# A fused attention and two-MLP kernel: state products 64 columns at a time, scores over the update in PSUM, and tile 0 in another order

## The chip, the core and the metric

The kernel runs on one core of a Trainium2 chip. The metric is the device time of one execution in microseconds (us); times are medians over runs. The engines are PE (TensorE, matrix products), PEld (its weight loads), DVE (VectorE), ACT (ScalarE), POOL (GpSimd) and SP (SyncE, which here only issues DMAs). Each works through its own queue in program order and waits for the others through semaphores.

## The reference

A gated linear attention over 4 batches, 8 heads, 768 tokens, head size 32 and state size 16, then two MLPs of width 256 to 2048 to 256 on the 3072 tokens.

```python
for c in range(nc):                       # chunks of the sequence
    cum = np.cumsum(la, axis=-1)
    L = np.exp(cum[:, :, :, None] - cum[:, :, None, :]) * causal
    M = np.einsum('bhin,bhjn->bhij', Cc, Bc) * L
    y_intra = np.einsum('bhij,bhjd->bhid', M, xc)
    y_inter = np.einsum('bhin,bhnd->bhid', Cc, state) * np.exp(cum)[:, :, :, None]
    y[:, :, sl] = y_intra + y_inter
    state = decay_full * state + sum_j(B_j x_j * decay_from_j)
...
h = np.maximum(x @ w_in, 0.0);  x = h * h @ w_out              # first MLP
h = x @ w_in2;  out = (h * np.clip(h + 3, 0, 6) / 6) @ w_out2  # second MLP
```

## The kernel before

The tokens stand as 6 tiles of 512 (128 tokens of each batch). Every large product is made from a high and a low part of both operands, in three terms: high by high, low by high, high by low. The attention runs in 12 *levels* of 64 tokens for all batches and heads; two levels make one tile.

The first MLP is a loop over tiles t = 0..5 and 16 blocks f = 0..15 of the hidden width. One pass is a *step* (t, f), written out by `step` (line 553). It puts into the queues, in this order: `mm1` (line 513, six matmuls of 512 columns) into one of two PSUM buffers; ACT's relu (522); in tile 0 for the blocks in `SQUARE` also ACT's square (524); `ready`, the splitting of a weight half into its high part on ACT (470) and its low part on POOL (472); DVE's square where ACT did not make it (528); the *burst*, attention work on PE; `mm2` of the step two before (546, six matmuls); ACT's high part `gha` (530); the *mid*, attention work of the other engines and, in tile 0, the decoding of a weight half; DVE's low part `gla` (532), which `mm2` of this step needs two steps later.

One level l of the attention is:

- `scale` (282, POOL): the rows B and C times their decays; `head` (291, ACT): C by head into `cb`; `tok` (297, POOL): B by token times its decay.
- `state` (PE, burst): a new tile `att` of four PSUM banks; `inter` (328), C by the state, into columns 256 to 383 (`y`), and `update` (356), B by x, into `u`, columns 384 to 511.
- `chunk` (PE, burst): `intra` (342), the masked scores of this level by x, added to `y`; then `scores` (308) of the level l+1 into columns 0 to 255 of the same tile.
- `high` (382, ACT) and `low` (387, DVE): `y` copied out as the high and low part of the MLP's input.
- `adv` (367 and 369, DVE): the next state from `u` and the old one.
- `mask` (316, DVE): the scores of the next level copied under the causal mask into `mt`, two banks in each of two instructions.

The tile `att` has one buffer only: `state` of level l+1 writes where `mask` l+1 reads the scores and `high`, `low` and `adv` of level l read `y` and `u`. The scheduler puts semaphore waits between accesses of two engines to one bank of one tile.

The order is written out by hand. `PLAN` says which of these stand at which step of tiles 0 to 2. From level 4 on a level has four steps: at 4l `mask` l, `tok` l and `scale` l+1; at 4l+1 `head` l+1; at 4l+2 `state` l; at 4l+3 `chunk`, `high`, `adv` and the loads of level l+2; at 4l+4 `low`. In tile 0 `JOIN1` says at which step a weight half j is decoded on DVE (`join`: `sign` 433, `bits` 438, `merge` 443), after ACT's `early` (429) a step before and ahead of its split a step later. Halves 2f' and 2f'+1 are the first and second MLP matrix of blocks 2f' and 2f'+1. A raw half of 512 KB comes by DMA (418) into places that the activations use later (halves 2 to 9) or into a ring of two buffers `raw` (the others).

Of the kernel before, what the change touches and what calls it, by code (L numbers as in the profile page):

```python
# [18 lines left out]
P = 128  # L19
NB = 4  # L20
H = 8
HD = 32
# [6 lines left out]
CH = 64  # L29
G = 256  # L30
# [12 lines left out]
NQUAD = NPAIR * NQ  # L43
LASTATT = 2

PLAN = {0: {0: ("upd1", "scale2"), 1: ("load3", "adv1", "head2"), 3: ("first2", "scale3"),
            4: ("mask2", "tok2", "head3"), 5: ("state2",), 6: ("chunk2", "adv2"), 7: ("high2", "load4"), 8: ("low2",),
            9: ("mask3", "tok3", "scale4"), 10: ("head4",), 11: ("state3",), 12: ("chunk3",), 13: ("high3", "load5"),
            14: ("low3", "gammas0"), 15: ("adv3",)}}
for _l in range(4, 12):  # L50
    for _k, _v in ((0, (f"mask{_l}", f"tok{_l}", f"scale{_l + 1}")), (1, (f"head{_l + 1}",)), (2, (f"state{_l}",)),
                   (3, (f"chunk{_l}", f"high{_l}", f"adv{_l}", f"load{_l + 2}")), (4, (f"low{_l}",))):
        _d = PLAN.setdefault((4 * _l + _k) // 16, {})
        _f = (4 * _l + _k) % 16
        _d[_f] = _v + _d.get(_f, ()) if _k == 4 else _d.get(_f, ()) + _v

JOIN1 = {0: 4, 1: 5, 2: 6, 3: 7, 5: 8, 6: 9, 7: 10, 8: 11, 10: 12, 11: 13, 12: 14, 13: 15}

SQUARE = (0, 2, 3, 5, 6, 7, 8, 9, 11)
QKEEP = 3
QNEW = 4

# [8 lines left out]
def attn_mlp_mlp(ctx: ExitStack, tc, a, bT, cT, bK, x, w1i, w1o, w2i, w2o, yT):  # L73


    nc = tc.nc
# [18 lines left out]
    act_h, act_l = {}, {}  # L95
# [147 lines left out]
    lev = [dict() for _ in range(NLEV)]  # L243
    state = {}

    def load(l, ec=nc.sync, eb=nc.sync):
        if l >= NLEV:
            return
        lev[l]["bc"] = t = at2.tile([P, NB, 2, CH], F32, tag="bc", name=f"bc{l}")
        for i, (eng, src) in enumerate(((ec, cT), (eb, bT))):  # L250
            eng.dma_start(out=t[:, :, i], in_=src.rearrange("p (b s) -> p b s", b=NB)[:, :, l * CH:l * CH + CH])

    def load_x(l, ex=nc.sync, eb=nc.sync):
        if l >= NLEV:
            return
        lev[l]["xb"] = t = at2.tile([P, 2, DM + P], F32, tag="xb", name=f"xb{l}")
        for eng, src, cols in ((eb, bK, slice(DM, DM + P)), (ex, x, slice(0, DM))):
            for r in range(2):
                eng.dma_start(out=t[CH * r:CH * r + CH, :, cols],
                              in_=src.rearrange("t (b l) w -> t b l w", b=NB)[:, 2 * r:2 * r + 2, l, :])  # L260

    def load_ef(l):
        if l >= NLEV:
            return
        s, k = divmod(l, CPG)
        lev[l]["ef"] = e = at2.tile([P, NB, 2 * CH], F32, tag="ef", name=f"ef{l}")
        nc.sync.dma_start(out=e.rearrange("p b t -> p (b t)"), in_=scr[k, s].rearrange("h b w t -> h (b w t)")
                          .unsqueeze(1).broadcast_to([H, NS, 2 * G]))

    def load_all(l):  # L270
        load(l)
        load_x(l)
        load_ef(l)

    def scale(l, eng=None):

# [40 lines left out]
                                      tri.bitcast(U32).unsqueeze(1).unsqueeze(1).broadcast_to([P, 2, NB, CH]),  # L317
                                      sc[:, q].rearrange("p k (z i) -> p k z i", i=CH))

    def inter(l, m=HD):  # L320

        y, d = lev[l]["y"], lev[l]
        for b in range(NB):
            for p in range(NPR):
                q, (r, c) = slice(32 * p, 32 * p + 32), divmod(b, 2)
                for e in range(0, 2 * HD, m):
                    o = CH * (p % 2) + e
                    nc.tensor.matmul(out=y[o:o + m, 2 * r + p // 2, c * CH:c * CH + CH],  # L328
                                     lhsT=state["S"][q, b, e:e + m], rhs=d["bc"][q, b, 0], start=c == 0,
                                     stop=False, skip_group_check=True)  # L330

    def intra(l):

# [39 lines left out]
    def operand(l, k):  # L373

        return act(l // 2, k).rearrange("p k (b l i) -> p k b l i", b=NB, l=2)[:, :, :, l % 2]

    def outputs(l, r):
        return lev[l]["y"][:, 2 * r:2 * r + 2].rearrange("p k (c i) -> p k c i", c=2)

    def evac_h(l):  # L380
        for r in range(2):
            nc.scalar.copy(out=operand(l, "h")[:, :, 2 * r:2 * r + 2], in_=outputs(l, r))

    def evac_l(l):
        for r in range(2):
            hi, lo = (operand(l, k)[:, :, 2 * r:2 * r + 2] for k in "hl")
            nc.vector.tensor_tensor(out=lo, in0=outputs(l, r), in1=hi.bitcast(F32), op=ALU.subtract)  # L387

    def place(l, t):
        lev[l].update(t=t, y=t[:, :, G:G + P], u=t[:, :, G + P:])  # L390

    def from_state(l):

# [11 lines left out]
    class Weights:  # L405
# [4 lines left out]
            self.raw, self.low, self.wt, self.v, self.hi, self.lo = {}, {}, {}, {}, {}, {}  # L410

        def dma(self, j):
            if self.pre == "a" and 2 <= j < 10:
                t, k = ((1, "h"), (2, "h"), (3, "h"), (3, "l"), (4, "h"), (4, "l"), (5, "h"), (5, "l"))[j - 2]
                raw = actp.tile([P, 2, 256, 2], U32, tag=f"{k}{t}", name=f"rawa{j}")
            else:
                raw = stagep.tile([P, 2, 256, 2], U32, tag="raw", name=f"raw{self.pre}{j}", bufs=2)
            nc.sync.dma_start(out=raw, in_=self.src[j % 2][:, j // 2].bitcast(U32).rearrange("p k (n w) -> p k n w", w=2))
            self.raw[j] = raw.rearrange("p k n w -> p (k n) w")
# [82 lines left out]
    w = {}  # L502
    pend = []

    def mm1(pre, t, f):
        ih, il, _, _ = w[pre].parts
        fb, fo = divmod(f, 2)
        pool, tag = (ps_y, "y") if 16 * t + f >= 52 and f % 4 > 1 else (ps_h, "h")
        h = pool.tile([P, TOK], F32, tag=tag, name=f"h{pre}{t}_{f}")
        i = 0  # L510
        for k in range(2):
            for wt, xt in ((ih, act_h), (il, act_h), (ih, act_l)):
                nc.tensor.matmul(out=h, lhsT=wt[fb][:, k, fo * P:fo * P + P], rhs=xt[t][:, k, :],  # L513
                                 start=i == 0, stop=i == 5)
                i += 1
        return h

    def gate(pre, t, f, h):
        gh = mlpp.tile([P, TOK], F32R, tag="gh", name=f"gh{pre}{t}_{f}", bufs=3)
        gl = mlpp.tile([P, TOK], F32R, tag="gl", name=f"gl{pre}{t}_{f}", bufs=3)  # L520
        g = mlpp.tile([P, TOK], F32, tag="g", name=f"g{pre}{t}_{f}")
        nc.scalar.activation(out=g, in_=h, func=AF.Relu)  # L522
        if t == 0 and f in SQUARE:
            nc.scalar.activation(out=g, in_=g, func=AF.Square)
            yield
        else:
            yield
            nc.vector.tensor_tensor(out=g, in0=g, in1=h, op=ALU.mult)  # L528
        yield
        nc.scalar.activation(out=gh, in_=g, func=AF.Copy)  # L530
        yield
        nc.vector.tensor_tensor(out=gl, in0=g, in1=gh.bitcast(F32), op=ALU.subtract)  # L532
        yield gh, gl
# [19 lines left out]

    def step(pre, t, f, ready=None, mid=None):

        gt = gate(pre, t, f, mm1(pre, t, f))
        next(gt)
        if ready:
            ready()
        next(gt)  # L560
        if t <= LASTATT + 1:
            burst_of(t, f)
        if len(pend) == LAG:
            mm2(*pend.pop(0))
        next(gt)
        if mid:
            mid(t, f)
        pend.append((pre, t, f, *next(gt)))
# [217 lines left out]
    w1 = w["a"] = Weights(w1i, w1o, "a")  # L786
# [52 lines left out]
    evac_h(0)  # L839
    evac_l(0)  # L840
    place(1, ps_a.tile([P, NPR, TOK], F32, tag="att", name="att1"))
    inter(1, 2 * HD)
    intra(1)
    w1.join(1)
    w1.early(2)
    w1.join(2)
    evac_h(1)
    evac_l(1)
    w1.split(1)
    w1.early(3)  # L850
    w1.split(2)
    w1.join(3)
# [13 lines left out]
    def attention(t, f, on_pe):  # L866
        for nm in PLAN.get(t, {}).get(f, ()):
            k = nm.rstrip("0123456789")
            l = int(nm[len(k):])
            if (k in ("state", "chunk", "first", "upd")) == on_pe and (l < NLEV or k in ("load", "scale", "head")):  # L870
                does[k](l)

    def burst_of(t, f):
        attention(t, f, True)
# [3 lines left out]
    def ready():  # L878

        if todo:  # L880
            x, j = todo.popitem()
            x.split(j)

    def decode(plan, f):
        if f in plan:
            w1.join(plan[f])
            todo[w1] = plan[f]
        if f + 1 in plan and plan[f + 1] not in w1.v:
            w1.early(plan[f + 1])
# [3 lines left out]
    def mid_first(t, f):  # L893
        attention(t, f, False)
        decode(JOIN1, f)
        for j in {0: (6, 7), 1: (8,), 2: (9,), 3: (10, 11), 7: (12,), 8: (13,), 10: (14,), 11: (15,)}.get(f, ()):
            w1.dma(j)

    def mid(t, f):
        attention(t, f, False)  # L900
        run(16 * t + f, 0)
# [92 lines left out]
```

## Time and profile before

| | |
|---|---|
| median of 3 runs | 584.66 us (584.62 to 585.59) |
| the profiled execution: its time | 586.12 us |
| the profiled execution: span of the trace | 584.4 us |
| PE busy | 562.1 us, 96% |
| DVE busy | 420.2 us, 72% |
| ACT busy | 359.3 us, 61% |
| POOL busy | 143.1 us, 24% |

How to read it: a busy share is an average over the span. The question for each stretch is whether PE waits there, and for whom. PEclk is the granted clock of PE: 1.00 is 2.4 GHz and 0.50 is 1.2 GHz. In the timeline the start and the duration are followed by the instruction; in square brackets stands the idle time of the engine before it, and what ended that. A matmul's duration contains the drain of the array, so the pace of a row of matmuls is read from start to start.

### The profile page before, as it was taken

The numbers are of one execution on the slowest core, as the hardware profiler recorded it, in microseconds if no ns is written. First come the engines' busy times: TensorE is split into PE (matmuls) and PEld (weight loads), VectorE is DVE, ScalarE is ACT, GpSimd is POOL, SyncE is SP. The second block draws the span as 40 slices with busy tenths as digits, with TensorE's granted clock in tenths as the row PEclk, the third lists the DMA queues.
The fourth block names the chain that finished last, engine by engine and source line by source line (L and its number), as shares of the span: only waits on it lengthen the run. The fifth ranks groups of instructions, "written<-read, shape, count | busy, mean of one in ns | idle before, by whom it ended". The sixth has DMA issues, their size and how long they took to land.

```text
span 584.4 us, 11106 instructions
## 1 busy us (share of the span) xinstructions
PE 562.1 (96%) x4451; PEld 449.4 (77%) x4451; DVE 420.2 (72%) x663; ACT 359.3 (61%) x624; POOL 143.1 (24%) x195
## 2 busy tenths in 40 slices
PE   7789899999999999999999899999999999999996
PEld 4457677777777888888887688888788888788885
DVE  6896786665565677667776876887867878676774
ACT  4576645444444565665665776777766777666663
POOL 6372550111210144344247400330000600000000
PEclk9799999999999999999999999999999999999999
DMA  8863412222240122122211000000200000200002
GB/s 239 224 211 101 127 47 60 70 65 66 65 136 3 37 73 60 49 72 73 72 37 36 1 1 1 1 0 1 72 1 1 1 1 0 72 1 0 1 1 73
DMA packets 32803, 31.47 MB, mean 54 GB/s; under 512 B 14608, under 2 KB 27376, under 8 KB 32752
## 3 DMA queue, kind: packets, MB, share of 16 engines
q1 hardware_dynamic: 30352, 29.85, 17.9%
q10 hardware_dynamic: 2400, 0.92, 0.6%
q8 instruction: 35, 0.57, 0.4%
q14 instruction: 16, 0.13, 0.1%
HBM read 27.41 MB, written 3.35 MB: 53 GB/s over the span
## 4 chain that ended last, share of the span: by engine, by line
PE 84%; POOL 4%; DVE 4%; ACT 3%; issue 3%; DMA 2%; POOLq 0%; DVEq 0%; ACTq 0%
PE y L691 22%; PE ha L513 19%; PE ya L546 18%; PE X L646 11%; PE Z L646 6%; PE V L646 3%; PE att L342 1%; DMA rawa<-in_w1o 1%; POOL al L472 1%; PE att L328 1%; PE att L308 1%; ACT ga L522 1%; POOL wtb L452 1%; PE att L356 1%; POOL bl L498 1%
## 5 line engine op out<-in xcount | busy, mean ns | idle before, releaser
L532 DVE TENSOR_TENSOR gla<-ga,gha 128x512 fp32r<-128x512 f32 x96 | 75.6, 787 | 32.3 <-ACT gha L530 32.0
L530 ACT ACTIVATE gha<-ga 128x512 fp32r<-128x512 f32 x96 | 60.6, 632 | 60.3 <-DVE ga L528 60.3
L522 ACT ACTIVATE ga<-ha 128x512 f32<-128x512 f32 x96 | 56.9, 593 | 61.1 <-PE ha L513 60.8
L528 DVE TENSOR_TENSOR ga<-ga,ha 128x512 f32<-128x512 f32 x87 | 59.6, 685 | 41.9 <-ACT ga L522 41.6
L513 PE MATMUL ha<-act_h,ah 128*128 128x512 f32 x192 | 76.2, 397 | 2.6 <-ACT ah L470 1.7
L513 PE MATMUL ha<-act_l,ah 128*128 128x512 f32 x192 | 76.1, 396 | 2.7 <-DVE act_l L387 2.7
L546 PE MATMUL ya<-gha,ah 128*128 128x512 f32 x192 | 77.9, 406 | 0.0
L513 PE MATMUL ha<-act_h,al 128*128 128x512 f32 x192 | 76.2, 397 | 0.8 <-POOL al L472 0.8
L546 PE MATMUL ya<-gla,ah 128*128 128x512 f32 x192 | 75.7, 394 | 1.4 <-DVE gla L532 1.4
L546 PE MATMUL ya<-gha,al 128*128 128x512 f32 x192 | 75.2, 392 | 0.0
L677 DVE TENSOR_TENSOR glc<-c,ghc 128x512 fp32r<-128x512 f32 x96 | 67.6, 706 | 5.7 <-ACT ghc L674 4.3
L668 DVE SCALAR_TENSOR_TENSOR c<-rc,c 128x512 f32<-128x512 f32 x72 | 50.9, 708 | 23.7 <-ACT rc L660 23.4
L660 ACT ACTIVATE rc<-c,three 128x512 f32<-128x512 f32 x72 | 52.0, 722 | 24.7 <-DVE c L655 24.5
L691 PE MATMUL y<-ghc,bh 128*128 128x512 f32 x168 | 65.5, 390 | 0.0
L691 PE MATMUL y<-glc,bh 128*128 128x512 f32 x168 | 65.4, 389 | 0.0
L691 PE MATMUL y<-ghc,bl 128*128 128x512 f32 x168 | 65.4, 389 | 0.0
L674 ACT ACTIVATE ghc<-c 128x512 fp32r<-128x512 f32 x96 | 58.7, 630 | 3.4 <-DVE c L668 3.2
L655 DVE TENSOR_TENSOR c<-Z,u 128x512 f32<-128x512 f32 x48 | 33.1, 690 | 22.8 <-PE Z L646 22.0
L513 PEld LDWEIGHTS ha<-act_h,ah 128*128 128x128 f32 x192 | 36.6, 191 | 11.3 <-ACT ah L470 2.5
L513 PEld LDWEIGHTS ha<-act_l,ah 128*128 128x128 f32 x192 | 36.8, 191 | 10.6 <-DVE act_l L387 3.1
L546 PEld LDWEIGHTS ya<-gla,ah 128*128 128x128 f32 x192 | 36.3, 189 | 10.6 <-DVE gla L532 3.0
L513 PEld LDWEIGHTS ha<-act_h,al 128*128 128x128 f32 x192 | 36.6, 191 | 9.8 <-POOL al L472 2.2
(297 smaller groups left out, 1022.6 us busy)
## 6 DMA issues: line engine op xcount, KB each, us to landing
rawa<-in_w1i SPq DMA_DIRECT2D x8, 512.0 KB
rawa<-in_w1o SPq DMA_DIRECT2D x8, 512.0 KB
rawb<-in_w2i SPq DMA_DIRECT2D x8, 512.0 KB
rawb<-in_w2o SPq DMA_DIRECT2D x8, 512.0 KB
xb<-in_x SPq DMA_DIRECT2D x24, 128.0 KB
ef<-scr SPq DMA_DIRECT2D x10, 256.0 KB
out_yT<-xf SPq DMA_DIRECT2D x10, 256.0 KB
bc<-in_cT SPq DMA_DIRECT2D x12, 128.0 KB
```

The lines of the kernel that those rows point to most:

```text
L513: nc.tensor.matmul(out=h, lhsT=wt[fb][:, k, fo * P:fo * P + P], rhs=xt[t][:, k, :], start=i == 0, stop=i == 5)
L522: nc.scalar.activation(out=g, in_=h, func=AF.Relu)
L528: nc.vector.tensor_tensor(out=g, in0=g, in1=h, op=ALU.mult)
L530: nc.scalar.activation(out=gh, in_=g, func=AF.Copy)
L532: nc.vector.tensor_tensor(out=gl, in0=g, in1=gh.bitcast(F32), op=ALU.subtract)
L546: nc.tensor.matmul(out=ys[m], lhsT=terms[i][0][fb][:, fo, m * P:m * P + P], rhs=terms[i][1], start=f == 0 and i == 0, stop=f == NF - 1 and ...
L646: nc.tensor.matmul(out=self.ps[bank], lhsT=lhsT, rhs=rhs, start=start and i == 0, stop=stop and i == 2, skip_group_check=True)
L660: nc.scalar.activation(out=self.sb["r" + c], in_=src, func=AF.Relu, bias=three)
L668: nc.vector.scalar_tensor_tensor(out=self.sb[c], in0=self.sb["r" + c], scalar=6.0, in1=src, op0=ALU.min, op1=ALU.mult)
L674: nc.scalar.activation(out=self.gh[c], in_=self.sb[c], func=AF.Copy)
L677: nc.vector.tensor_tensor(out=self.gl[c], in0=self.sb[c], in1=self.gh[c].bitcast(F32), op=ALU.subtract)
L691: nc.tensor.matmul(out=ys[t][m], lhsT=terms[i][0][:, 7 + 2 * (1 - f) + m], rhs=terms[i][1], start=first and i == 0, stop=last and i == 2, ...
```

## The change

`inter` always takes 64 columns of the state in one product (before: 32 at a time, except at level 1, which the call `inter(1, 2 * HD)` ran at 64). `u` moves to columns 0 to 127 of `att`, where `scores` of the next level are put later, so `adv` of a level has to be ahead of its `chunk` in the plan. From level 4 on a level now runs: 4l `state` and `scale` l+1; 4l+1 `adv` and `head` l+1; 4l+2 `chunk` and `tok` l+1; 4l+3 `mask` l+1, `high`, `low` and the loads. In tile 0 `PLAN`, `JOIN1`, `SQUARE` and the steps of the weight DMAs change, halves 12 to 15 land in the places of halves 6 to 9, `mm1` of step (0, 0) takes its two terms with the low input last, and ahead of the loop `low` of level 1 comes before the merge of half 1 and the decoding of half 2. `load_all` issues `ef` ahead of `x`.

```diff
-PLAN = {0: {0: ("upd1", "scale2"), 1: ("load3", "adv1", "head2"), 3: ("first2", "scale3"),
-            4: ("mask2", "tok2", "head3"), 5: ("state2",), 6: ("chunk2", "adv2"), 7: ("high2", "load4"), 8: ("low2",),
-            9: ("mask3", "tok3", "scale4"), 10: ("head4",), 11: ("state3",), 12: ("chunk3",), 13: ("high3", "load5"),
-            14: ("low3", "gammas0"), 15: ("adv3",)}}
+PLAN = {0: {0: ("upd1", "scale2"), 1: ("adv1", "load3", "head2"), 3: ("first2", "scale3", "gammas0"), 4: ("mask2", "tok2"),
+            5: ("head3",), 6: ("state2",), 7: ("adv2", "tok3"), 8: ("chunk2",), 9: ("mask3", "high2", "low2", "load4"),
+            11: ("state3", "scale4"), 12: ("adv3", "head4"), 13: ("chunk3",),
+            14: ("tok4", "mask4", "high3", "low3", "load5")}}
 for _l in range(4, 12):
-    for _k, _v in ((0, (f"mask{_l}", f"tok{_l}", f"scale{_l + 1}")), (1, (f"head{_l + 1}",)), (2, (f"state{_l}",)),
-                   (3, (f"chunk{_l}", f"high{_l}", f"adv{_l}", f"load{_l + 2}")), (4, (f"low{_l}",))):
...
+    for _k, _v in ((0, (f"state{_l}", f"scale{_l + 1}")), (1, (f"adv{_l}", f"head{_l + 1}")), (2, (f"chunk{_l}", f"tok{_l + 1}")),
+                   (3, (f"mask{_l + 1}", f"high{_l}", f"low{_l}", f"load{_l + 2}"))):
...
-JOIN1 = {0: 4, 1: 5, 2: 6, 3: 7, 5: 8, 6: 9, 7: 10, 8: 11, 10: 12, 11: 13, 12: 14, 13: 15}
-SQUARE = (0, 2, 3, 5, 6, 7, 8, 9, 11)
+JOIN1 = {0: 4, 1: 5, 2: 6, 3: 7, 4: 8, 5: 9, 6: 10, 7: 11, 8: 12, 10: 13, 11: 14, 13: 15}
+DMA1 = {0: (6, 7), 1: (8,), 2: (9,), 3: (10, 11), 4: (12,), 5: (13,), 6: (14,), 8: (15,)}
+SQUARE = (0, 2, 3, 4, 6, 8, 10, 11, 13)
...
     def load_all(l):
         load(l)
+        load_ef(l)
         load_x(l)
-        load_ef(l)
...
-    def inter(l, m=HD):
+    def inter(l):
...
-                for e in range(0, 2 * HD, m):
-                    o = CH * (p % 2) + e
-                    nc.tensor.matmul(out=y[o:o + m, 2 * r + p // 2, c * CH:c * CH + CH],
-                                     lhsT=state["S"][q, b, e:e + m], rhs=d["bc"][q, b, 0], start=c == 0,
-                                     stop=False, skip_group_check=True)
+                o = CH * (p % 2)
+                nc.tensor.matmul(out=y[o:o + CH, 2 * r + p // 2, c * CH:c * CH + CH], lhsT=state["S"][q, b],
+                                 rhs=d["bc"][q, b, 0], start=c == 0, stop=False, skip_group_check=True)
...
-        lev[l].update(t=t, y=t[:, :, G:G + P], u=t[:, :, G + P:])
+        lev[l].update(t=t, y=t[:, :, G:G + P], u=t[:, :, 0:P])
...
-            if self.pre == "a" and 2 <= j < 10:
-                t, k = ((1, "h"), (2, "h"), (3, "h"), (3, "l"), (4, "h"), (4, "l"), (5, "h"), (5, "l"))[j - 2]
+            if self.pre == "a" and j >= 2 and j not in (10, 11):
+                t, k = ((1, "h"), (2, "h"), *((t, k) for t in (3, 4, 5) for k in "hl"))[j - 2 if j < 10 else j - 8]
...
-        gt = gate(pre, t, f, mm1(pre, t, f))
+        gt = gate(pre, t, f, mm1(pre, t, f, *(() if t or f else ((0, 1, 3, 4, 2, 5),))))
...
-    inter(1, 2 * HD)
+    inter(1)
     intra(1)
-    w1.join(1)
-    w1.early(2)
-    w1.join(2)
+    w1.sign(1)
+    w1.bits(1)
     evac_h(1)
     evac_l(1)
+    w1.merge(1)
+    w1.early(2)
     w1.split(1)
+    w1.join(2)
     w1.early(3)
...
-        for j in {0: (6, 7), 1: (8,), 2: (9,), 3: (10, 11), 7: (12,), 8: (13,), 10: (14,), 11: (15,)}.get(f, ()):
+        for j in DMA1.get(f, ()):
             w1.dma(j)
```

## Rows read from the trace of the kernel before

**Rows 1.** Busy time by stage: stretch, length, then busy us of each engine, PEclk, DMA share.

```profile
20.04:84.63 64.59, 56.45 (x629) 41.96 (x630) 52.86 (x81) 42.56 (x78) 33.79 (x41) 0.89 0.52 145
84.63:195.00 110.37, 110.37 (x1858) 87.22 (x1857) 66.58 (x113) 51.41 (x99) 15.93 (x20) 1.00 0.22 62
```

**Rows 2.** Waits of PE from 20 to 200 us: total, times, longest.

```profile
PE att L328 <- issue: 2.9, 1, 2.9
PE ha L513 <- DVE act_l L387: 2.7, 1, 2.7
PE ha L513 <- ACT ah L470: 1.7, 1, 1.7
...
PE ha L513 <- POOL al L472: 0.8, 3, 0.3
```

**Rows 3.** Busy time by stage, columns as in rows 1, behind two waits of PE.

```profile
42.00:48.00 6.00, 5.09 (x106) 4.08 (x107) 3.91 (x7) 3.85 (x8) 1.87 (x3) 0.72 0.21 48
70.00:74.00 4.00, 3.83 (x101) 2.41 (x100) 1.80 (x3) 2.23 (x4) 1.66 (x3) 0.58 0.53 155
```

**Rows 4.** Timeline of PE: the state products at 64 columns, then at 32.

```profile
17.71 0.69 PE L328 MATMUL att<-bc,S 32*64 32x64 f32 x32 [0.80 <-DVE S L369]
18.34 0.86 PE L342 MATMUL att<-mt,xb 64*32 64x64 f32 x64
...
104.96 0.39 PE L513 MATMUL ha<-act_l,ah 128*128 128x512 f32 x1
105.28 0.85 PE L328 MATMUL att<-bc,S 32*32 32x64 f32 x64
106.07 0.45 PE L356 MATMUL att<-xb 64*32 64x64 f32 x32
```

**Rows 5.** Timeline of two steps of tile 1, all engines.

```profile
113.44 0.39 PE L513 MATMUL ha<-act_l,ah 128*128 128x512 f32 x1
...
114.56 0.69 DVE L528 TENSOR_TENSOR ga<-ga,ha 128x512 f32<-128x512 f32 x1 [0.95 <-ACT ga L522]
115.03 0.39 PE L513 MATMUL ha<-act_h,ah 128*128 128x512 f32 x1
115.16 0.75 DVE L387 TENSOR_TENSOR act_l<-att,act_h 128x256 fp32r<-128x256 f32 x2
115.83 1.36 DVE L316 COPY_PREDICATED mt<-tri,att 128x512 f32<-128x512 uint32 x2
116.16 0.39 PE L513 MATMUL ha<-act_l,ah 128*128 128x512 f32 x1
```

**Rows 6.** Timeline: `high` and `low` of level 0.

```profile
17.69 0.65 ACT L382 CAST act_h<-yu 128x256 fp32r<-128x256 f32 x2 [3.93 <-DVE S L369]
18.37 0.76 DVE L387 TENSOR_TENSOR act_l<-yu,act_h 128x256 fp32r<-128x256 f32 x2 [0.71 <-ACT act_h L382]
```

**Rows 7.** Waits of DVE, 85 to 200 us: total, times, longest.

```profile
DVE S L367 <- ACT act_h L382: 8.6, 7, 1.2
```

**Rows 8.** DVE by line, 19 to 88 us: count, busy us, mean ns, idle before.

```profile
L532 DVE TENSOR_TENSOR gla<-ga,gha 128x512 fp32r<-128x512 f32 x16 | 13.2, 825 | 0.8 <-ACT gha L530 0.8
L443 DVE SCALAR_TENSOR_TENSOR wta<-wta,lowa 128x512 uint32<-128x512 uint32 x15 | 12.2, 813 | 1.4
L438 DVE TENSOR_SCALAR lowa<-rawa 128x512 uint16<-128x512 uint16 x15 | 9.9, 662 | 0.5
L433 DVE TENSOR_SCALAR lowa<-rawa 128x512 uint32<-128x512 uint32 x15 | 9.4, 627 | 0.1
...
L369 DVE TENSOR_TENSOR S<-S,gam 128x256 f32<-128x256 f32 x3 | 2.3, 772 | 0.1
...
L367 DVE TENSOR_TENSOR S<-att,S 128x256 f32<-128x256 f32 x3 | 1.3, 418 | 4.1 <-PE att L308 4.1
L233 DVE TENSOR_SCALAR gam<-gl,hm 128x32 f32<-128x32 f32 x2 | 1.2, 672 | 0.0
L230 DVE TENSOR_TENSOR gl<-gl 128x44 f32<-128x44 f32 x1 | 0.7, 735 | 0.0
```

More of the change, by code (lines that the diff above doesn't have):

```diff
@@ L44 @@
 LASTATT = 2
-PLAN = {0: {0: ("upd1", "scale2"), 1: ("load3", "adv1", "head2"), 3: ("first2", "scale3"),
-            4: ("mask2", "tok2", "head3"), 5: ("state2",), 6: ("chunk2", "adv2"), 7: ("high2", "load4"), 8: ("low2",),
-            9: ("mask3", "tok3", "scale4"), 10: ("head4",), 11: ("state3",), 12: ("chunk3",), 13: ("high3", "load5"),
-            14: ("low3", "gammas0"), 15: ("adv3",)}}
+PLAN = {0: {0: ("upd1", "scale2"), 1: ("adv1", "load3", "head2"), 3: ("first2", "scale3", "gammas0"), 4: ("mask2", "tok2"),
+            5: ("head3",), 6: ("state2",), 7: ("adv2", "tok3"), 8: ("chunk2",), 9: ("mask3", "high2", "low2", "load4"),
+            11: ("state3", "scale4"), 12: ("adv3", "head4"), 13: ("chunk3",),
+            14: ("tok4", "mask4", "high3", "low3", "load5")}}
 for _l in range(4, 12):
-    for _k, _v in ((0, (f"mask{_l}", f"tok{_l}", f"scale{_l + 1}")), (1, (f"head{_l + 1}",)), (2, (f"state{_l}",)),
-                   (3, (f"chunk{_l}", f"high{_l}", f"adv{_l}", f"load{_l + 2}")), (4, (f"low{_l}",))):
-        _d = PLAN.setdefault((4 * _l + _k) // 16, {})
-        _f = (4 * _l + _k) % 16
-        _d[_f] = _v + _d.get(_f, ()) if _k == 4 else _d.get(_f, ()) + _v
-JOIN1 = {0: 4, 1: 5, 2: 6, 3: 7, 5: 8, 6: 9, 7: 10, 8: 11, 10: 12, 11: 13, 12: 14, 13: 15}
-SQUARE = (0, 2, 3, 5, 6, 7, 8, 9, 11)
+    for _k, _v in ((0, (f"state{_l}", f"scale{_l + 1}")), (1, (f"adv{_l}", f"head{_l + 1}")), (2, (f"chunk{_l}", f"tok{_l + 1}")),
+                   (3, (f"mask{_l + 1}", f"high{_l}", f"low{_l}", f"load{_l + 2}"))):
+        PLAN.setdefault((4 * _l + _k) // 16, {})[(4 * _l + _k) % 16] = _v
+JOIN1 = {0: 4, 1: 5, 2: 6, 3: 7, 4: 8, 5: 9, 6: 10, 7: 11, 8: 12, 10: 13, 11: 14, 13: 15}
+DMA1 = {0: (6, 7), 1: (8,), 2: (9,), 3: (10, 11), 4: (12,), 5: (13,), 6: (14,), 8: (15,)}
+SQUARE = (0, 2, 3, 4, 6, 8, 10, 11, 13)
 QKEEP = 3
@@ L503, in attn_mlp_mlp, with mm1 @@
     pend = []
-    def mm1(pre, t, f):
+    def mm1(pre, t, f, order=(0, 1, 2, 3, 4, 5)):
         ih, il, _, _ = w[pre].parts
@@ L509, in mm1 @@
         h = pool.tile([P, TOK], F32, tag=tag, name=f"h{pre}{t}_{f}")
[L510 to L515, printed above, removed]
+        terms = [(k, wt, xt) for k in range(2) for wt, xt in ((ih, act_h), (il, act_h), (ih, act_l))]
+        for i, (k, wt, xt) in enumerate(terms[n] for n in order):
+            nc.tensor.matmul(out=h, lhsT=wt[fb][:, k, fo * P:fo * P + P], rhs=xt[t][:, k, :], start=i == 0, stop=i == 5)
         return h
```

## The prediction

> **What bounds the kernel now.** I read the busy time by stage first. In tile 0 (20.04 to 84.63 us, ahead of the first matmuls of tile 1) PE is busy 56.45 of 64.59 us at a mean clock of 0.89, and DVE 52.86 us; from there to 195 us PE is busy without a gap at full clock, and DVE, ACT and POOL have room [rows 1]. So whatever PE saves in tiles 1 and 2 is saved in full, and whatever PE must wait for there is lost in full; in tile 0 PE and DVE hold each other up. Second, the waits of PE: 2.9 us ahead of `state` 2, 2.7 us for the low input of step (0, 0), 1.7 us for weight half 12 [rows 2]. The list has no wait of PE in tiles 1 and 2. Third, what such a wait brings with it: behind the 2.9 us the granted clock falls to its lower level (0.50) for a while; over 42 to 48 us its mean is 0.72, so 6 x 0.28 = 1.7 us of full clock are lost. Behind the 1.7 us wait it is 0.58 over 4 us, again 1.7 us [rows 3]. Behind a wait of 0.80 us it does not: the 64 `intra` products that follow at 18.34 us last 0.86 us, full rate [rows 4].
>
> **Part 1, 64 columns.** At 32 columns a level has 64 PE instructions, 105.28 to 106.07 us: 0.79 us from first start to the start of `update`. Level 1 already runs at 64 columns: 32 instructions, 17.71 to 18.34, 0.63 us, at full clock [rows 4]. So an instruction gets dearer (20 against 12 ns) and the gain is 0.16 us a level; eight levels (4 to 11) lie where PE is saturated: -1.3 us. The other bound is that halving the instructions halves the time: 0.39 us a level, -3.1 us; I take the row of the form itself.
>
> The Trainium skill's page "TensorEngine Tiling (Array Packing)", section on performance considerations (instruction overhead), says that a matmul costs about 60 cycles whatever its free dimension below that; with 64 columns of moving data this would make the instruction count the price, and the part would be worth -3.1 us. The trace speaks against it: the level 1 row is 0.63 us, not 0.39.
>
> **Part 2, the new order in tiles 1 and 2.** `mask` l+1, `high` l and `low` l now stand at the mid of step 4l+3, and `state` l+1, which overwrites the buffer that all three read, at the burst of step 4l+4, the very next. Before, `state` came two steps behind `mask` and three behind `high`. I measure everything from the start of the last matmul of `mm1` of step 4l+3; the step at 113.44 us stands for it [rows 5]. PE: `mm2`, then the next `mm1`, whose matmuls start from 115.03 to 116.16 (six paces of 0.226, so 1.36 us for an `mm1` or an `mm2`), and 0.32 us for the change to `inter`, as at 104.96 to 105.28 [rows 4]: PE is ready at 3.04. DVE: its square starts at 1.12 and the next instruction at 1.72 [rows 5], so `mask` runs from 1.72 to 3.08 (1.36 us). Then ACT's `high`. Both only read the tile, but readers of one tile on two engines are also put one behind the other here: `high` of level 0 stood idle for 3.93 us until DVE's `adv` had read, and `low` starts after both halves of `high` have ended (17.69 + 0.65 to 18.37) [rows 6]; in tiles 1 and 2 `adv` waits for `high` seven times, 8.6 us in all [rows 7]. So `high` runs from 3.12 to 3.75 (0.03 us from an end to a start, 0.65 us), `low` from 3.78 to 4.53 (0.75 us), and `state` starts at 4.58. PE is ready at 3.04: it waits 1.54 us. Nothing covers it, PE has no other work queued; behind `state` it is `update`, `mm2` and the next `mm1` that come late. It happens at levels 5 to 11, seven times (`mask` 4 is at step 14 of tile 0, two steps ahead): +10.8 us. Bounds: if `high` ran beside `mask`, `low` would end at 3.83 - 0.02 and the wait would be 0.8 us, 7 x 0.8 = +5.6; nothing in rows 6 and 7 supports that, so I take 1.54.
>
> `adv` ahead of `chunk`, and the scores that overwrite `u`: `chunk` now waits for `adv`. By the same offsets `adv` ends 1.72 + 0.42 + 0.42 = 2.6 us behind the reference point of step 4l+1, PE reaches `chunk` at 3.04: covered by 0.4 us, nothing. `head` l+1 stays one step ahead of the scores that need it, where no wait stands now: nothing. `tok` moves two steps ahead of its `state`; on SP `ef` is issued ahead of `x`, so `scale` gets it earlier, and no PE wait of before was for it [rows 2]: nothing.
>
> Clock: the new gaps of 1.54 us lie between the 0.80 us without and the 1.7 us with a fall of the clock. From none to all seven cost 1.7 us each, 0 to +11.9 us. It is nearer to the gap that did fall, but that one had small waits for the low part of the same half (POOL, up to 0.3 us) just behind it [rows 2]; I take one fall, +1.7, and keep the ends.
>
> **Part 3, tile 0.** The low input of level 1 gets ready 2.9 us sooner (`low` no longer stands behind a merge and a whole decoding, 0.81 + 2.10), so the 2.7 us wait goes. But DVE then has no pause: I follow its queue from 18.37 us to the end of `adv` 2, which `chunk` 2 now needs. Ahead of it stand the decodings of half 1 to half 10, ten, at 2.10 us (0.63 + 0.66 + 0.81), seven `gla` at 0.83 [rows 8], three squares at 0.69 [rows 5], `low` 0 and 1 (1.5), `adv` 1 and 2 (0.42 + 0.77 each, 2.4), `mask` 2 (1.4) and `gammas` (2 x 0.67 + 0.74 = 2.1, moved from step 14 to step 3): 21.0 + 5.8 + 2.1 + 7.4 = 36.3 us. Some 50 instructions start up to 0.08 us ahead of the end of the one before (115.16 + 0.75 against 115.83); at 0.05 that is 2.5 us off, and `adv` 2 ends at 18.37 + 33.8 = 52.2; with a pause or two I take 52.5. `adv` 2 itself now has `state` 2 two steps ahead and no longer idles (4.1 us) for the end of `chunk` [rows 8]. `state` 2 itself moves one step later, behind `mask` 2 (about 42 us) and `tok` 2, so its 2.9 us wait goes too, and what PE has done by 52.5 us is everything up to `mm1` 8. From `chunk` 2 on PE has no late operand: half 12 is now decoded at step 8 and not 10 (the 1.7 us wait goes), and `gla` 6 to 13 are ready by 1 us or more. PE needs `chunk` 2 (1.5), eight `mm2` and seven `mm1` at 1.36 (20.4), `state` 3 (1.1), `chunk` 3 with a short wait for `adv` 3 (2.0): 25.0 us. So tile 1 starts at 77.8 us (with 0.3 us of pauses) instead of 84.6: -6.8 us. DVE then has `low` 3 ready at about the third matmul of tile 1, no wait. The raw halves 12 to 15 wait for places that are free since step 3 to 5: issued earlier, and no one waited long for them before. Bounds: DVE never pausing at all would give 20.04 + 52.86 + 1.4 (`mask` 4, now inside) = 74.3, -10 [rows 1]; a fall of the clock at the waits that stay (`mm2` of step 3 for `gla` 3, about 2 us, `chunk` 2 for `adv` 2 up to 2 us), with 1.5 us more on DVE, -3.5.
>
> **Sum.** Tile 0 -6.8, products -1.3, waits ahead of `state` +10.8, clock +1.7: +4.4 us. The profiled execution took 586.12 us (584.4 in the trace and 1.7 around it), 1.46 above the median of 584.66; from the median: 589.1 us.
>
> **The rivals.**
> (a) The clock falls behind most of the seven gaps: four to seven falls, +9.5 to +14.6: 594 to 599 us. For: the 1.7 us wait. Against: 0.80 us did nothing.
> (b) The other side: `high` does not wait for `mask`, since both only read. Then the gap is 0.8 us, no fall of the clock, -6.8 - 1.3 + 5.6 = -2.5: 582 us. It decides from a gap under 1.16 us, where seven of them are 8.1. For: only `low` needs `high`. Against: rows 6 and 7.
> (c) The new order doesn't hold PE at all, because DVE and ACT are further ahead there than in the step I read: -8.1, 576.5 us. Against: the square of the step itself needs `mm1` of that step, and nothing ahead of it can make `mask` earlier.
> (d) Tile 0 gets all that DVE allows (-10), or the products are worth their count, with the gaps as forecast: 584 to 586 us, no difference.
>
> **How the numbers follow.** The forecast 0.42 (586 to 592.5), (a) 0.18, (b) 0.18, (c) 0.09, (d) 0.13. About 0.2% (1.2 us) is what a measurement can tell from no change. Faster: (b) and (c), 0.27; same: most of (d) and the low edge of the forecast, 0.13; slower 0.60. The range leaves out (c) and the upper part of (a): 580 to 597 us.
>
> **What would show it.** In the trace of the changed kernel: `inter` 32 instructions in 0.63 us up to `update`; PE idle about 1.5 us ahead of `inter` of levels 5 to 11, released by `low`, with `mask`, `high`, `low` one behind the other; a level of four steps longer by 1.4 us than before; the first `mm1` of tile 1 near 78 us; no wait for half 12. Wrong would be: `high` beginning under `mask`; PE without gaps in tiles 1 and 2; tile 1 starting after 81 or before 75 us.

## The result, and the profile after

The changed kernel takes 592.51 us (median of 6 runs, 590.78 to 600.61), the kernel before 584.80 us beside it: a ratio of 1.012, 95% interval 1.0104 to 1.0135, so slower by 1.2%. Two of the six runs, at 600.5 and 600.6 us, and one of a later kernel, at 600.7 us, lie apart from the rest and are left out of the ratios and of all that follows; the other four here have a median of 592.1 us. The profiled execution took 592.02 us (span 590.3). The forecast was 589.1 us, with a range of 580 to 597.

The line numbers of the changed kernel: `inter` 327, `update` 354, `intra` 340, `scores` 308, `mask` 316, `high` 380, `low` 385, `adv` 365 and 367, `sign`, `bits` and `merge` 431, 436 and 441, split (POOL) 470, `mm1` 510, `gla` 527, `mm2` 541.

Busy time by stage of the changed kernel (columns as in [rows 1]), tile 0 from its first `mm1` to that of tile 1, then up to the same place at step (3, 0):

```profile
19.91:80.29 60.38, 53.76 (x564) 40.15 (x565) 54.75 (x84) 43.08 (x79) 33.36 (x41) 0.93 0.54 156
80.29:200.65 120.36, 109.56 (x1602) 86.26 (x1600) 63.89 (x109) 50.27 (x96) 16.28 (x21) 1.00 0.20 56
```

Before, tile 0 took 64.43 us (20.04 to 84.47) and tiles 1 and 2 110.35 us, with PE busy throughout. So tile 0 gained 4.1 us, and tiles 1 and 2 lost 10.0; behind 200.65 us both kernels need the same, 389.6 us. Where PE waits in the changed kernel, 20 to 205 us:

```profile
PE att L327 <- issue: 10.8, 7, 1.6
PE ya L541 <- DVE gla L527: 4.4, 4, 1.8
PE att L340 <- DVE S L365: 1.7, 1, 1.7
```

All three lines are new, and the first is nearly all of the loss. [rows 2] had no wait in tiles 1 and 2; its three long waits are gone. The waits of `mm2` for `gla` (second line, all between 29 and 50 us) and of `chunk` 2 for `adv` 2 (third line) lie in tile 0. One of the seven waits, with all that leads up to it, in the timeline of the changed kernel (in square brackets the idle time before, and what ended it):

```profile
108.99 0.69 DVE L523 TENSOR_TENSOR ga<-ga,ha 128x512 f32<-128x512 f32 x1 [2.28 <-ACT ga L517]
109.59 1.36 DVE L316 COPY_PREDICATED mt<-tri,att 128x512 f32<-128x512 uint32 x2
110.59 0.39 PE L510 MATMUL ha<-act_l,ah 128*128 128x512 f32 x1
110.99 0.65 ACT L380 CAST act_h<-att 128x256 fp32r<-128x256 f32 x2 [0.65 <-DVE mt L316]
111.67 0.76 DVE L385 TENSOR_TENSOR act_l<-att,act_h 128x256 fp32r<-128x256 f32 x2 [0.71 <-ACT act_h L380]
112.53 0.69 PE L327 MATMUL att<-bc,S 32*64 32x64 f32 x32 [1.54 <-issue]
113.15 0.45 PE L354 MATMUL att<-xb 64*32 64x64 f32 x32
```

Read down the starts: square, `mask`, `high`, `low`, `inter`, each at the end of the one before, on three engines. PE's last matmul of `mm1` began at 110.59, and PE had nothing more to do. "issue" names no engine; that it is `low` is read from its end at 112.43, 0.10 us ahead of `inter`, and the experiments below bear it out. `inter` itself takes 0.62 us up to `update` (0.79 before, [rows 4]).

### The profile page after: what moved, and what is told of

It is laid out like the page before. It is cut to its first block, busy times and chain, and to the rows that moved or that the text cites. A ratio compares the mean times of both kernels' runs of the same rounds, so it can differ in the third digit from the quotient of the medians.

```text
span 590.3 us, 10468 instructions
## 1 busy us (share of the span) xinstructions
PE 557.2 (94%) x4131; PEld 446.1 (76%) x4131; DVE 420.1 (71%) x663; ACT 359.2 (61%) x624; POOL 143.0 (24%) x195
## 4 chain that ended last, share of the span: by engine, by line
PE 83%; DVE 7%; issue 4%; ACT 2%; POOL 2%; DMA 1%; SPq 0%; DVEq 0%; ACTq 0%; POOLq 0%
PE y L686 22%; PE ya L541 19%; PE ha L510 18%; PE X L641 11%; PE Z L641 6%; PE V L641 3%; PE att L340 2%; PE att L327 1%; DVE gla L527 1%; PE att L308 1%; DVE ga L523 1%; DMA xb<-in_x 1%; DVE lowa L436 1%; DVE mt L316 1%; PE att L354 1%
## 5 line engine op out<-in xcount | busy, mean ns | idle before, releaser
L541 PEld LDWEIGHTS ya<-gha,ah 128*128 128x128 f32 x192 | 36.2, 188 | 10.1 <-issue 1.5
L496 POOL TENSOR_TENSOR bl<-wtb,bh 128x256 fp32r<-128x256 f32 (+1 forms) x42 | 34.7, 859 | 33.8 <-ACT bh L489 33.8
```

What stands on the lines that cost most here:

```text
L541: nc.tensor.matmul(out=ys[m], lhsT=terms[i][0][fb][:, fo, m * P:m * P + P], rhs=terms[i][1], start=f == 0 and i == 0, stop=f == NF - 1 and ...
```

## The experiments

Each stands beside the changed kernel ("after", 592.1 us) and beside runs of the kernel before on the same chip (585.2 to 585.5 us). They ran on three chips, and "after" was not run again on them: a difference of about 1 us between kernels of two chips is at the edge of what these runs can tell.

**32 columns again.** Is a product worth what the row of level 1 said?

```diff
-    o = CH * (p % 2)
-    nc.tensor.matmul(out=y[o:o + CH, ...], lhsT=state["S"][q, b], ...)
+    for e in range(0, 2 * HD, HD if l > 1 else 2 * HD):
+        o, m = CH * (p % 2) + e, HD if l > 1 else 2 * HD
+        nc.tensor.matmul(out=y[o:o + m, ...], lhsT=state["S"][q, b, e:e + m], ...)
```

> The changed kernel with the state products of levels 2 to 11 in 32 columns again, nothing else. My theory (a 64-column product is dearer, 0.63 against 0.79 us a level): eight levels in tiles 1 and 2 get 0.16 us longer, +1.3 us over the changed kernel, some 593.5 us; the two in tile 0 cost nothing or 0.3 us. Rival (the instruction count is the price): +0.39 us a level, +3.1 us, some 595.3 us. Third case (nothing is gained, because the time goes into the drain behind the products): no difference, 592.2 us. The waits of PE ahead of the state products stay 1.54 us in all three.

Measured: 598.12 us (595.70 to 599.73), ratio 1.0219 [1.0183, 1.0256]. From the start of one `inter` to the next are 15.50 us in three of the first five periods (15.68 in the first, 15.53 in the fourth), against 15.36 in after: 0.14 us for 32 instructions more. But the last levels take longer. The timeline of PE, and the busy time by stretch behind the gaps that end at 127.17 and at 158.20 us:

```profile
111.67 0.84 PE L328 MATMUL att<-bc,S 32*32 32x64 f32 x64 [1.53 <-issue]
127.17 0.84 PE L328 MATMUL att<-bc,S 32*32 32x64 f32 x64 [1.53 <-issue]
...
158.20 0.84 PE L328 MATMUL att<-bc,S 32*32 32x64 f32 x64 [1.53 <-issue]
175.34 0.84 PE L328 MATMUL att<-bc,S 32*32 32x64 f32 x64 [1.55 <-issue]
```

```profile
129.00:131.00 2.00, 2.00 (x11) 1.61 (x10) 0.66 (x1) 0.00 (x0) 0.00 (x0) 1.00 0.62 134
...
160.00:162.00 2.00, 2.00 (x7) 1.52 (x6) 0.68 (x1) 0.00 (x0) 0.00 (x0) 0.50 0.57 127
162.00:164.00 2.00, 2.00 (x7) 1.62 (x6) 0.00 (x0) 0.00 (x0) 0.00 (x0) 0.65 0.42 137
```

Both gaps are 1.53 us. Behind the first the granted clock stays at 1.00 (2.4 GHz), behind the second it is 0.50 (1.2 GHz), and PE gets 7 matmuls through in 2 us instead of 11. The period with such a fall is 17.14 us: 1.64 us more (the next one 17.10). It fell behind the last three of the seven gaps; in the profile of after behind none. From the first `inter` of tile 1 to the end of the profile this kernel takes 6.2 us more than after: eight times 0.14 us and three falls are 6.0. The forecast of 593.5 us had no fall in it.

**The copies one step earlier.** If the chain `mask`, `high`, `low` is the wait, then `high` and `low` of levels 4 to 11, put at step 4l+2, take it away whole:

```diff
-  ... (2, (f"chunk{_l}", f"tok{_l + 1}")), (3, (f"mask{_l + 1}", f"high{_l}", f"low{_l}", f"load{_l + 2}"))
+  ... (2, (f"chunk{_l}", f"tok{_l + 1}", f"high{_l}", f"low{_l}")), (3, (f"mask{_l + 1}", f"load{_l + 2}"))
```

> The changed kernel with the two output copies (high, low) of levels 4 to 11 one step earlier, in the step of the chunk; the mask stays where it is. My theory (the wait ahead of state is the chain of mask, high and low behind the square of the step before): only the mask is left in it, it ends 3.08 us behind the last matmul of mm1 and PE is ready at 3.04, so the seven waits fall from 1.54 to some 0.1 us and the time by 7 x 1.45 = 10 us, to 582 us, under both kernels. Rival (PE is held by something else there, the update's operand or the loads): the waits stay and the time is 592 us. Rival (DVE gets late in the step of the chunk instead, its gla arrives late): the waits move to mm2, 585 to 592 us.

Measured: 581.14 us (580.09 to 582.13), ratio 0.9927 [0.9909, 0.9945]. Timeline of this kernel:

```profile
94.53 1.35 DVE L316 COPY_PREDICATED mt<-tri,att 128x512 f32<-128x512 uint32 x2
...
95.53 0.39 PE L510 MATMUL ha<-act_l,ah 128*128 128x512 f32 x1
95.98 0.69 PE L327 MATMUL att<-bc,S 32*64 32x64 f32 x32
```

`inter` shows no idle time ahead of it, since the matmul's modelled drain covers what is left; but it starts 0.45 us behind the last `mm1` matmul and not 0.32, right at the end of `mask` (95.88). The change thus contains 11 us that it need not have paid, and without them it is faster than the kernel before.

**The mask twice.** If PE is released by that chain, a second masked copy in it is as much more of wait. In `mask`:

```diff
+        if 5 <= l < NLEV:
+            ks = ks + ks
```

> The changed kernel with the masked copy of levels 5 to 11 made twice (the same values once more, 1.3 us of DVE each): a disputed cost doubled. My theory (the gap ahead of state is mask, high, low one behind the other): each of the seven gaps grows by 1.3 us, from 1.54 to 2.85 us, +9.1 us, 601 us if the clock does not fall. On the clock: with three of seven gaps of 1.54 us followed by half clock in the run with 32 columns and none in the profile of the changed kernel, gaps of 2.85 us should be followed by it nearly always, 1.64 us each: up to +11.5 us more, 613 us. Rival (mask is not in the chain, low follows high only): the gaps stay near 1.54 us, 592 us.

Measured: 614.55 us (614.11 to 615.0), ratio 1.0495 [1.0474, 1.0516]. Timeline of PE at four of the seven gaps, and the busy time by stretch behind the first three:

```profile
98.31 0.69 PE L329 MATMUL att<-bc,S 32*64 32x64 f32 x32 [2.75 <-issue]
...
116.48 0.91 PE L329 MATMUL att<-bc,S 32*64 32x64 f32 x32 [2.74 <-issue]
...
134.53 1.13 PE L329 MATMUL att<-bc,S 32*64 32x64 f32 x32 [2.74 <-issue]
...
153.85 0.75 PE L329 MATMUL att<-bc,S 32*64 32x64 f32 x32 [2.75 <-issue]
```

```profile
100.00:104.00 4.00, 4.00 (x13) 3.15 (x12) 0.69 (x1) 0.07 (x1) 0.00 (x0) 0.61 0.45 121
116.00:120.00 4.00, 3.52 (x69) 2.87 (x70) 2.27 (x5) 0.73 (x2) 0.00 (x0) 0.60 0.19 43
135.00:139.00 4.00, 4.00 (x66) 3.13 (x59) 1.32 (x3) 0.63 (x1) 0.00 (x0) 0.50 0.34 85
```

The gap grew by 1.21 us; the doubled copy takes 2.56 us, 1.20 more. And here the clock fell behind every one of the seven gaps. Without a fall a period would be 15.36 + 1.21 = 16.57 us. From 98.31 to 116.48 and on to 134.53 are 18.17 and 18.05, 1.5 to 1.6 us more; from 134.53 to 153.85 are 19.32, 2.75 more: that fall was a longer one. The six periods between the seven gaps lose 11.6 us to the clock. With 7 x 1.21 = 8.5 us of wait that is 20.1 of the 22.9 us between the two profiled spans; the fall behind the seventh gap, another long one (at 213 us the clock is still 0.50), accounts for the rest.

**32 columns without the gaps.** The copies early, and levels 4 to 11 at 32 columns, as in the first edit with `l > 3` for `l > 1`:

> The changed kernel with the copies high and low of levels 4 to 11 one step earlier, and besides the products of the state at levels 4 to 11 at 32 columns at a time again. It measures the products' share by itself, without the gaps ahead of the state. The same kernel with 64 columns took 581.1 us. If 64 columns are worth 0.16 us a level, as the level periods without a fall of the clock say, this one takes 8 x 0.16 = 1.3 us more: 582.4 us (581.9 to 583.0). Rival: halving the number of instructions halves the time (0.39 us a level): 584.3 us. Rival: 64 columns are worth nothing once PE is saturated, the shorter products being taken up by the matmuls around them: 581.1 us.

Measured: 583.30 us (582.38 to 584.03), ratio 0.9963 [0.9950, 0.9975]. `inter` of level 4 and of level 11 in its timeline, and in that of the kernel with 64 columns:

```profile
82.03 0.85 PE L328 MATMUL att<-bc,S 32*32 32x64 f32 x64
...
180.68 0.84 PE L328 MATMUL att<-bc,S 32*32 32x64 f32 x64
```

```profile
82.10 0.69 PE L327 MATMUL att<-bc,S 32*64 32x64 f32 x32
...
179.36 0.69 PE L327 MATMUL att<-bc,S 32*64 32x64 f32 x32
```

98.65 against 97.26 us for seven levels: 0.20 us a level, 1.6 us for eight. The medians are 2.2 us apart, on two chips, and this one lies 0.3 us above the range that was forecast; the two profiled spans are 1.5 apart. So 64 columns gain 0.14 to 0.20 us a level, not nothing and not 0.39.

**Tile 0: which step is late?** Five kernels on the order of tile 0. First `gammas` back from step 3 to step 8, in after and in the kernel with early copies:

```diff
-  3: ("first2", "scale3", "gammas0"), ... 8: ("chunk2",)
+  3: ("first2", "scale3"), ... 8: ("chunk2", "gammas0")
```

> The changed kernel with gammas0 (three DVE instructions, 1.7 us, which only adv 3 needs) at step 8 of tile 0 and not at step 3. My theory of the gain in tile 0 that fell short (DVE's queue holds adv 2 and with it chunk 2 until 53.8 us, PE waits 1.74 us and the clock falls behind it): adv 2 comes 1.7 us earlier, the 1.74 us wait is gone or under 0.3 us, the clock does not fall at 54 us, and tile 1 starts some 3.4 us earlier (77 against 80.3 us): 588.8 us. If only the wait goes and the clock falls elsewhere: 590.5 us. Rival (another engine holds chunk 2): the wait stays, 592 us, or 594 if the gammas hold up step 8.

> Both edits, copies early and gammas late. If the two causes are separate and additive: 592.2 - 10 - 3.4 = 578.8 us, 6 us under the kernel before. If one of the waits only hides the other: 582 us, as with the copies alone.

Measured: 591.24 us (590.68 to 592.75), ratio 1.0105 [1.0083, 1.0128], and 580.93 us (580.18 to 581.66), 0.9924 [0.9907, 0.9941]: 0.9 and 0.2 us below the kernels without the edit, with overlapping intervals. The gain of 3.4 us that was forecast did not come. The waits of PE in tile 0, first of the edit in after:

```profile
PE att L340 <- DVE S L365: 1.7, 1, 1.7
PE att L308 <- issue: 1.2, 1, 1.2
```

`chunk` 2 waits as long as it did: `adv` 2 begins at 52.31 us (53.36 in after), and what PE does ahead of `chunk` 2 moves earlier with it, since PE is held there by `gla` 3 on the same engine. And where the clock does not fall behind that 1.7 us wait, as here, the scores of level 4 wait 1.2 us for `scale` 4, which stands behind POOL's splitting of half 13. That gave the next edit, on top of both:

```diff
-  ... 11: ("state3", "scale4"), ...
+  ... 10: ("scale4",), 11: ("state3",), ...
```

> Both edits (e4) and scale 4 one step earlier in tile 0, at step 10. In the traces of e2, e3 and e4 the scores of chunk 3 wait 1.16 to 1.19 us, behind scale 4 on POOL, which stands in its queue behind the low part of half 13. My theory (when the clock's fall behind chunk 2 is gone, this wait takes its place): the wait is gone, tile 1 starts 1.2 us earlier, 579.7 us against 580.9. Rival (the next one, the head or gla 11, takes its place at once): 580.9 us.

Measured: 580.02 us (579.66 to 580.53), ratio 0.9908 [0.9891, 0.9924]. Its waits of PE, 50 to 84 us:

```profile
PE att L340 <- DVE S L365: 1.2, 1, 1.2
PE att L327 <- PE ha L510: 0.8, 1, 0.8
PE att L308 <- POOL al L470: 0.2, 1, 0.2
```

The scores' wait went from 1.2 to 0.2 us, and the median fell by 0.9, with overlapping intervals. Then, on the kernel with early copies alone, two edits, each by itself. The start ahead of the loop as before (the calls written in one line):

```diff
-    w1.sign(1)  w1.bits(1)  evac_h(1)  evac_l(1)  w1.merge(1)  w1.early(2)  w1.split(1)  w1.join(2)
+    w1.join(1)  w1.early(2)  w1.join(2)  evac_h(1)  evac_l(1)  w1.split(1)
```

> The kernel with the early copies (e2), with the start of before: half 1 merged and half 2 decoded ahead of the low copy of level 1. My theory (tile 0 is held by DVE's queue from the start to adv 2): the low input is ready 2.9 us later and PE waits 2.7 us in step (0, 0), but DVE's work is only in another order, so chunk 2 starts at the same distance from the start, and the time stays within 1 us of 581.1. Rival (PE's early waits go through to the end): +2.7 us or, with the clock's fall behind them, +4.4 us, 584 to 585.5 us.

Measured: 580.11 us (579.72 to 580.52), ratio 0.9907 [0.9892, 0.9921]: 1.0 us below the kernel with the new start, where the forecast was no more than 1 us of difference. `low` 1 is then late again, by 0.8 us ahead of the terms of `mm1` (0, 0) that need it, and PE's mean granted clock from 20 to 30 us is 0.52 and not 0.68; but PE's waits for `gla` fall from 4.1 to 2.0 us, and `adv` 2 begins at 52.69 and not at 53.83.

The places of the raw halves as before:

```diff
-DMA1 = {..., 4: (12,), 5: (13,), 6: (14,), 8: (15,)}
+DMA1 = {..., 6: (12,), 8: (13,), 9: (14,), 11: (15,)}
-            if self.pre == "a" and j >= 2 and j not in (10, 11):
+            if self.pre == "a" and 2 <= j < 10:
```

> The kernel with the early copies (e2), with raw halves 12 to 15 in the ring of two buffers again, their DMAs issued at steps 6, 8, 9 and 11. The half 12 then can only be issued when half 10 is decoded (about 50 us), lands some 4 us later and is needed by ACT at 54 and DVE at 57 us. My theory (these places only take away waits of SP, PE has 1 us or more to spare here): 0 to +1 us, 581 to 582 us. Rival (the places are what lets half 12 be decoded at step 8): the decoding of half 12 waits 2 us or more and everything behind it on DVE too, 583 to 585 us.

Measured: 583.29 us (581.97 to 584.79), ratio 0.9963 [0.9949, 0.9977]: 2.1 us slower with the old places, more than the forecast. Tile 0 is 60.83 us long against 59.37. But the decoding of half 12 is not late, so the rival's reason is not it either. The wait of `chunk` 2 is 1.74 us instead of 1.16, and a fall of the clock follows it: the last `merge` ahead of `adv` 2 takes 1.28 us instead of 0.69. The profile of after shows the same 1.74 us, the same `merge` and the same fall with the new places (last section). So that the places are worth the 2.1 us is not shown.

**What helped, together.** Early copies, late `gammas`, early `scale` 4 and the old start:

> The combination of what helped: copies of levels 4 to 11 one step earlier, gammas at step 8, scale 4 at step 10, and the start ahead of the loop as in the kernel before. The start as before was worth -1.0 us on one version (581.1 to 580.1). If that gain adds up with the others, this takes 579.0 us (578.5 to 579.8). Rival: the start's gain and that of the later gammas are one and the same pause of DVE's queue, and don't add up: 580.0 us.

Measured: 579.04 us (578.85 to 579.22), ratio 0.9893 [0.9878, 0.9908]: the fastest of all, as forecast, and tile 0 is 57.05 us long. The old start gives 1.0 us here too.

Not tried: 64 columns alone, in the order of the kernel before. What a product is worth is known from pairs in the new order only.

## Why the prediction was right, and where it was off

In profiled spans the change costs 5.9 us (584.4 to 590.3), where the sum said 4.4. The medians lie 7.3 us apart (584.8 and 592.1), because the profiled execution of before was 1.3 us above its median and that of after 0.1 below. That the sum came so near is in part luck: tile 0 gained some 2.6 us less than forecast, and the fall of the clock that was allowed for ahead of `state`, 1.7 us, did not come in the profile.

- **The waits ahead of `state`, +10.8.** Right, in number, place, cause and size. From the last `mm1` matmul to `inter` are 1.94 us, of which 0.32 would have been there anyway: 1.6 us, forecast 1.54. `high` did wait for `mask` (0.65 us idle), though both only read, and that decides between 1.5 and 0.8 us. The Trainium skill's page "PSUM — Partial Sum Buffer", section "PSUM bank collisions raise a hardware error", asks for an order here: two engines must not touch one bank and quadrant at once, two reads included. The trace agrees in that `high` waits; what would happen without the wait no run here shows.
- **The products, -1.3.** Right: 0.14 us a level in one pair of kernels, 0.20 in the other, 0.16 taken from [rows 4]. The 60 cycles for each matmul of the Trainium skill's page "TensorEngine Tiling (Array Packing)", section "Instruction Overhead", read as a price by count, would have given 0.39 (an estimate); no pair shows that. The periods of a level close the sum: before 13.92, less 0.16, plus 1.61, is 15.37; measured 15.36. With early copies it is 13.89: 0.13 us a level are left, `mask` alone.
- **The clock, +1.7.** The mechanism was right; that one fall would come was a guess within the spread. Gaps of 1.53 to 1.55 us were followed by a fall in three of seven cases in one kernel, and in none in the profiles of after and of after with late `gammas`; at 2.75 us in all seven. So rival (a) was no other mechanism, but the same one with other luck: the kernel with 32 columns drew part of it. One fall was found behind `chunk` 2 (below). And the reading that a wait of 0.80 us brings no fall does not hold in general. Timeline of PE in the changed kernel:

```profile
16.88 0.46 PE L327 MATMUL att<-bc,S 32*64 32x64 f32 x16 [0.80 <-DVE S L367]
17.54 0.52 PE L327 MATMUL att<-bc,S 32*64 32x64 f32 x16 [0.20 <-issue]
17.99 1.18 PE L340 MATMUL att<-mt,xb 64*32 64x64 f32 x64
```

  Behind these two waits the clock is 0.50 from 18 to 24.5 us, and `intra` takes 1.18 us and not 0.86. In before it is 0.50 from 23 to 29.5 us, behind the 2.7 us wait; the prediction's list of falls left that one out.
- **Tile 0, -6.8.** Too much: tile 1 starts at 80.29 (84.47 before), -4.2, not at 77.8. Two terms failed. First, DVE's queue "with a pause or two". The busy time was right (33.89 us from 18.37 to the end of `adv` 2 at 54.40; 33.8 forecast), but DVE also stood idle for 2.1 us, and 0.3 were allowed. The rows of DVE by line of the changed kernel, 18 to 54 us, have them in the last column:

```profile
L441 DVE SCALAR_TENSOR_TENSOR wta<-wta,lowa 128x512 uint32<-128x512 uint32 x10 | 8.7, 872 | 0.8
L436 DVE TENSOR_SCALAR lowa<-rawa 128x512 uint16<-128x512 uint16 x10 | 7.1, 707 | 0.3
L431 DVE TENSOR_SCALAR lowa<-rawa 128x512 uint32<-128x512 uint32 x10 | 6.3, 628 | 0.1
...
L385 DVE TENSOR_TENSOR act_l<-att,act_h 128x256 fp32r<-128x256 f32 x2 | 0.8, 419 | 0.8 <-ACT act_h L380 0.8
```

  0.8 us ahead of `low` for `high`, and 1.2 us in the ten decodings, most of it ahead of `merge`, which reads what `bits` has just written. [rows 8] had this: 1.4 + 0.5 + 0.1 us of idle time beside fifteen decodings, 0.13 each. The prediction added the means and left out that column. So `adv` 2 ended at 54.4 and not at 52.5, and `chunk` 2, which waits for its first instruction only, began at 53.82. Second, "from `chunk` 2 on PE has no late operand" forgot the bound that the text itself had named: the wait ahead of `chunk` 2 was 1.74 us, and the clock fell behind it.

```profile
54.00:56.00 2.00, 2.00 (x98) 1.64 (x85) 1.93 (x4) 1.78 (x4) 0.87 (x2) 0.84 0.08 27
56.00:58.00 2.00, 2.00 (x6) 1.52 (x6) 1.97 (x4) 1.16 (x2) 0.86 (x2) 0.50 0.21 60
58.00:60.00 2.00, 2.00 (x9) 1.59 (x8) 1.84 (x3) 0.11 (x1) 0.79 (x1) 0.81 0.47 137
```

  Busy time by stretch in the changed kernel: 2 x (0.16 + 0.50 + 0.19) = 1.7 us lost, so PE needed 26.5 us from `chunk` 2 to tile 1, not 25.0. A scores' wait of 1.2 us lay hidden behind that fall. This second part was luck too: the kernel with early copies has the same order in tile 0, and in its profile `chunk` 2 waits 1.16 us, no fall follows, and tile 0 is 59.37 us long. That is 5.1 us less than before, still short of 6.8.
- **Cost nothing:** `adv` ahead of `chunk` from level 4 on, `head`, `tok`, `ef` ahead of `x`: right, no wait of PE names them there. The new start was taken for a gain (the 2.7 us wait goes, and it did); undone, it gives 1.0 us in both pairs, and `adv` 2 begins 1.1 and 0.8 us earlier.
- **Rivals.** (b) fell with the order `mask`, `high`, `low`, (c) with the seven gaps; (d) with 0.14 to 0.20 us a level and -4.2.

## What to carry to other kernels

When a buffer with one copy gets overwritten one step earlier, add up every reader of it, across engines and one behind the other, from the last thing that the readers wait for: here that sum, made from the old trace, gave the wait to 0.1 us. Then ask which of the readers could have read sooner: moving two names in a plan turned a loss of 1.2% into a gain of 0.7%. And when an engine's queue is added up, the idle column of its rows belongs to the sum as much as the means.

## What the runs showed of the hardware

- The clock's fall is no fixed price of a gap. Behind gaps of 1.53 to 1.55 us in equal surroundings it came or did not come; behind 1.7 us ahead of `chunk` 2 it came in after and with the old places, and did not come with late `gammas` or with the old start. Falls of one kind cost 1.5 to 1.64 us each; three of the seven behind gaps of 2.75 us were longer, and the two of them that lie inside a full period cost 2.75 and 2.82 us.
- DVE is slower beside POOL, and not always by the same. Timeline of the changed kernel in tile 0, with POOL at rest and then beside its split:

```profile
40.68 0.69 DVE L441 SCALAR_TENSOR_TENSOR wta<-wta,lowa 128x512 uint32<-128x512 uint32 x1
41.29 0.68 DVE L527 TENSOR_TENSOR gla<-ga,gha 128x512 fp32r<-128x512 f32 x1
...
49.83 0.47 DVE L436 TENSOR_SCALAR lowa<-rawa 128x512 uint16<-128x512 uint16 x1
50.40 1.89 POOL L470 TENSOR_TENSOR al<-wta,ah 128x256 fp32r<-128x256 f32 x2 [2.61 <-ACT ah L468]
50.41 1.28 DVE L441 SCALAR_TENSOR_TENSOR wta<-wta,lowa 128x512 uint32<-128x512 uint32 x1
51.62 1.22 DVE L527 TENSOR_TENSOR gla<-ga,gha 128x512 fp32r<-128x512 f32 x1
```

  `merge` and `gla` take 0.69 and 0.68 us with POOL at rest, 1.28 and 1.22 beside the split. The Trainium skill's "GPSIMD Engine Reference", section "Specifications", says that the two share their SBUF interfaces, with contention where DVE has two SBUF inputs; both instructions have two, and the trace agrees. The same place in the kernel with early copies:

```profile
51.47 0.69 DVE L441 SCALAR_TENSOR_TENSOR wta<-wta,lowa 128x512 uint32<-128x512 uint32 x1
51.48 3.98 POOL L470 TENSOR_TENSOR al<-wta,ah 128x256 fp32r<-128x256 f32 x4 [2.61 <-ACT ah L468]
52.08 1.23 DVE L527 TENSOR_TENSOR gla<-ga,gha 128x512 fp32r<-128x512 f32 x1
```

  Here `merge` begins 0.01 us ahead of the split and takes 0.69 us. So it goes in all eleven profiles of the new order: where the split begins 0.01 to 0.02 us earlier (four of them), this `merge` takes 1.28 us and `chunk` 2 waits 1.70 to 1.74; where `merge` begins first or at the same time (seven), 0.69 and 1.12 to 1.16. No run sets which of the two begins first, so that this order is the cause is read from the traces and not shown by an experiment.
